# Cluster attention with gated projection on one core: paired sums of weight tiles on GpSimd, single-input work on ScalarE, and scaling straight out of the accumulator

## The chip, the cores and the metric

The kernel runs on one core of a Trainium2 chip. A core has five engines that run side by side, each through its own list of instructions in order: TensorE (matmuls and weight loads), VectorE, ScalarE, GpSimd and SyncE, which here issues the DMAs. They wait for one another by semaphores. The metric is the time of the program on the device in microseconds, lower is better; each execution gives one time. The program on record before the change was run three times.

## What is computed

Four batches, eight heads each, 768 positions, 64 features a head. Queries and keys are assigned to the nearest of 16 centroids; a query attends only to keys of its own cluster. The heads' outputs, put side by side (512 wide), go through a causal convolution of five taps whose sigmoid gates a projection, and a second projection gives the result.

```python
scores = scale * np.matmul(q, k.transpose(0, 1, 3, 2))
scores = np.where(mask, scores, -1000000000.0)
attn = np.exp(scores - np.max(scores, axis=-1, keepdims=True))
attn = attn / (np.sum(attn, axis=-1, keepdims=True) + 1e-09)
x = np.matmul(attn, v)                      # then heads side by side
gate = 1.0 / (1.0 + np.exp(-gate_pre))      # gate_pre: 5-tap convolution of x
out = gate * (x @ w_val) @ w_out
```

## The kernel before

**Heads and pairs.** There are 32 heads, worked on as 16 pairs, four to a batch. A head's scores are 768 x 768, made in six tiles of 128 keys x 768 queries. Each float operand is split into a high and a low part (`prep_x2`, `prep_x1` for one side, `prep_y1`, `prep_y2` for the other, L473 to L508) so that TensorE's faster float format is exact enough; the cluster one-hot rows lie in the low part and put the mask into the scores.

**A tile's way.** `qk` (L550) makes a score tile in PSUM (two buffers, `sp`). VectorE takes a maximum over each row (`rowmax`, L574), ScalarE the exponential (`expo`, L581), with the first tile's maximum as the shift for the whole head; the result is a weight tile `pt` of 128 x 768 floats in SBUF, one of 16 buffers. Two uses follow. `av` (L698) multiplies it with the values into an accumulator, both heads of a pair side by side, two banks a pair (one for each half of the queries). `sum_p` (L621) multiplies it with a block of weights 32 columns wide to get the row sums: one *set* is four matmuls, one for each head and half. `GROUPS` (L831) says which tiles a set covers; a group of two tiles is first added by `add_p` (L614) on GpSimd, into a buffer `ad`. Before the change every group has one tile, so no adds run and a pair has six sets. `weigh` and `weigh_v` (L588, L610) undo the shift between the keys' tiles by scaling the values.

**Scaling.** `av_out` (L711) copies the two banks of attention sums to `xr` on ScalarE and so frees them. `sum_out` (L635) copies the row sums out; a DMA gathers them (`sum_spread`), VectorE takes the reciprocals (`recip`), one DMA writes them to DRAM (`recip_row`) and two bring them back across partitions (`recip_rows`, tile `rs`). `scale_x` (L715) multiplies `xr` by `rs` on GpSimd. The last pair goes another way, over TensorE transposes.

**After the attention.** `post_x` and `post_xl` split x in high and low, `post_conv` (L730) does the five taps, the first on ScalarE or GpSimd (`scaled`), the other four on VectorE. `val` and `proj` (L780, L805) are the projections, which run on TensorE between the attention's matmuls; those of the last batch come at the end. The two weight matrices are decoded in the first part of the run (`load_w1`, `load_w3`).

**The order.** All instructions are in hand-made order: a planner written in Python (L829 to L1267) builds a list of operations `Op` with an engine (or a choice of engines, for the kinds in `FLEX`), a duration, predecessors, buffers to take and a due time, and simulates the engines greedily. Only the order and the choice of engine and buffer come out of it; on the chip the semaphores decide when each instruction runs. PSUM has four banks of the kind `acc`, shared by attention accumulators, row sums, projections and small transposes. When GpSimd and certain VectorE operations (`PORT`, L847) overlap in the plan, both are lengthened by `CLASH` = 0.8 of the overlap. TensorE's rule (L1179 on) prefers score tiles, up to three in a row, then alternates between bursts of attention products and of projections; sets of sums go ahead of attention products.

**The end.** A flag tells whether the fast path was exact enough; the program then branches over `general_path` (L1314), which these inputs don't take.

Of the kernel before, what the change touches and what calls it, by code (L numbers as in the profile page):

```python
# [14 lines left out]
ALU = mybir.AluOpType  # L15
# [139 lines left out]
def kernel(  # L155
# [12 lines left out]
    PE, V, S, G = nc.tensor, nc.vector, nc.scalar, nc.gpsimd  # L168

    NH, D, SQ = qT.shape  # L170
# [3 lines left out]
    NP = HB // 2  # L174
# [325 lines left out]

    def prep_y2(h, i):

        if ops[h][3] is None:
            ops[h][3] = operand(h, 3)
        y2 = ops[h][3]
        c = slice(i * HALF, (i + 1) * HALF)
        n = P if h < 2 else D
        (V if on[0] == "V" else G).tensor_tensor(y2[0:n, c], raws["k", h][0:n, c], ops[h][2][0:n, c].bitcast(F32), op=ALU.subtract)  # L508
# [206 lines left out]
    def scale_x(p, hf):  # L715
        if hf is None:
            x = xrs[p % 3][:, KW - 1:KW - 1 + SQ]
            G.tensor_tensor(x, x, sums.pop(p), op=ALU.mult)  # L718
        else:
            x = xrs[p % 3][:, KW - 1 + hf * HALF:KW - 1 + (hf + 1) * HALF]  # L720
            V.tensor_tensor(x, x, sums.pop((p, hf))[:, 0:HALF], op=ALU.mult)

# [48 lines left out]
    FLEX = ("X2", "Y1", "W1", "W3", "XF", "MQ", "PX", "PC0", "VS")  # L771
    CLASH = 0.8


# [54 lines left out]
    NS = 2 * NT  # L829
    NPT, NAD = 16, 4  # L830
    GROUPS = [[(t,) for t in range(NT)] for p in range(NPAIR)]  # L831
    NTILE = NH * NT
# [18 lines left out]
    class Op:  # L851
        def __init__(o, kind, eng, dur, f, *a, after=(), take=None, dl=None, lo=0, key=0):
            o.kind, o.engs, o.f, o.a = kind, eng if isinstance(eng, dict) else {eng: dur}, f, a
            if len(o.engs) > 1 and kind not in FLEX:
                o.engs = {"G": o.engs["G"]} if "G" in o.engs else {"V": o.engs["V"]}
            o.port = kind in PORT
            o.after = [x for x in after if x is not None]
            o.take, o.dl, o.lo, o.key, o.n = take, dl, lo, key, len(todo)
            o.end, o.got, o.users, o.on, o.free = None, 0, [], None, None
            todo.append(o)  # L860
# [67 lines left out]
    X1 = [Op("XF", {"G": 1.75, "V": 0.5}, 0, prep_x1_first, 1, hf * HALF, (hf + 1) * HALF, after=[X2], dl=2 + 5 * hf) for hf in range(2)]  # L928
    Y2 = [Op("Y2", "G", 0.97, prep_y2, 1, hf, after=[Y1], dl=2) for hf in range(2)]
    x10 = Op("X1", "V", 0.5, prep_x1, 0, HALF, SQ, dl=4)  # L930
# [22 lines left out]
    for h in range(2, NH):  # L953
# [6 lines left out]
        X1 = Op("X1", "V", 0.88, prep_x1, h, after=[X2], dl=s - 5).frees(LQ)  # L960
        Y2 = Op("Y2", "G", 0.97, prep_y2, h, 0, after=[Y1], dl=s - 5)
        Y2 = Op("Y2", "G", 0.97, prep_y2, h, 1, after=[Y2], dl=s - 5).frees(LK)
        ready[h] = [X1, Y2]

# [53 lines left out]
    for p in range(NPAIR):  # L1018
# [20 lines left out]
        prev.frees(LV[p])  # L1039
        for hf in range(2):  # L1040
            AVO[p, hf] = Op("AO", "A", 0.375, av_out, p, hf, after=[AVK[p, hf, NT - 1]], dl=-1).frees(AVK[p, hf, 0])
        LE = Op("LE", "A", 0.42, sum_out, p, after=[LL[p, len(GROUPS[p]) - 1]], take="lr", dl=-1).frees(LL[p, 0])
        if p < NPAIR - 1:
# [3 lines left out]
            RS = dma("RS", recip_rows, p, after=[RR], take="rs", dl=0).frees(RR)  # L1047
            SX[p, 0] = SX[p, 1] = Op("SX", "G", 1.65, scale_x, p, None, after=[AVO[p, 0], AVO[p, 1], RS], dl=-1).frees(RS)
        else:
            LT = Op("RT", "P", 0.33, sum_t, p, after=[LE], take="acc", dl=-1).frees(LE)  # L1050
            RQ = Op("RC", "V", 0.35, recip_q, p, after=[LT], dl=-1).frees(LT)
            late.append(LT)
            for hf in range(2):
                RB = Op("RB", "G", 0.6, recip_b, p, hf, after=[RQ], take="st", dl=-1)
                RT = Op("RT", "P", 0.33, recip_t, p, hf, after=[RB], take="acc", dl=-1).frees(RB)
                SX[p, hf] = Op("SV", "V", 0.46, scale_x, p, hf, after=[AVO[p, hf], RT], dl=-1).frees(RT)
# [82 lines left out]
    free = {"P": 0.0, "V": -0.2, "A": -0.2, "G": -0.6, "S": 0.5}  # L1139
    running = {"V": None, "G": None}  # L1140
    state = {"qk": 0, "since": 0, "last": None, "run": 0, "open": None}
# [10 lines left out]
    def est(o, e):  # L1152
# [6 lines left out]
        if o.take:  # L1159
# [3 lines left out]
            t = max(t, f[0])  # L1163
        return t

# [49 lines left out]
    while left:  # L1215
# [13 lines left out]
        T = max(T, est(o, e))  # L1229
        dur = o.engs[e]  # L1230
        if e == "P":

# [18 lines left out]
        o.start = T  # L1251
        if e in running:
            x = running["G" if e == "V" else "V"]
            if (o.port or e == "G") and x is not None and (x.port or x.on == "G") and x.free > T:
                m = CLASH * min(x.free - T, dur)
                dur, x.free, x.end, free[x.on] = dur + m, x.free + m, x.end + m, free[x.on] + m
            running[e] = o
        free[e] = o.free = T + dur
# [38 lines left out]
    prep_first2(0, 0)  # L1297
    prep_y2(0, 0)
    on[0] = "V"
    prep_y2(0, 1)  # L1300
    for t in range(2):
        qk(0, t, True)
    warm(WARM[3])
    for i, hf, e in ((0, 0, "A"), (1, 0, "V"), (1, 1, "V")):
        on[0] = e
        prep_mask0(0, i, hf)
    for o in order:
        got[0], on[0] = o.got, o.on
        o.f(*o.a)
# [3 lines left out]
    ctx.close()  # L1313
    with tc.If(rv != 0, preferred_fallthrough_block=False):  # L1314
        general_path(tc, qT, kT, v, out, cenT, cw, wsplit, ident)
# [39 lines left out]
```

## Time and profile before

| what | us |
|---|---|
| median of three runs | 588.81 |
| lowest and highest of them | 587.38, 590.2 |
| the profiled execution: its own time | 589.81 |
| the profiled execution: its span, first to last instruction | 588.1 |
| mean granted TensorE clock, share of full | 0.963 |

The profile shows one execution. *Busy* is the time in which an engine executes something; a matmul's end is modelled, and matmuls overlap. A row of a group gives line, engine, operation, tiles and shape, count, then busy time in us and mean duration in ns, then the idle time just before and what ended it. A row of waits says who waited for whom, us in total, how often, longest. A row of windows gives, for a stretch of the span, the busy time of each engine with the count of instructions, the granted clock, the DMA engines' share and GB/s. "PEld" is the weight load, a "q" behind an engine's name its sequencer. Where a line gathers several forms, a mean mixes them.

### The profile page before, as it was taken

The numbers are of one execution on the slowest core, as the hardware profiler recorded it, in microseconds if no ns is written. First come the engines' busy times: TensorE is split into PE (matmuls) and PEld (weight loads), VectorE is DVE, ScalarE is ACT, GpSimd is POOL, SyncE is SP. The second block draws the span as 40 slices with busy tenths as digits, with TensorE's granted clock in tenths as the row PEclk, the third lists the DMA queues.
The fourth block names the chain that finished last, engine by engine and source line by source line (L and its number), as shares of the span: only waits on it lengthen the run. The fifth ranks groups of instructions, "written<-read, shape, count | busy, mean of one in ns | idle before, by whom it ended". The sixth has DMA issues, their size and how long they took to land. (4 is left out here: it accounts for less than half of the span.)

```text
span 588.1 us, 8869 instructions
## 1 busy us (share of the span) xinstructions
PE 540.1 (92%) x3235; PEld 342.3 (58%) x3235; DVE 411.7 (70%) x582; ACT 298.8 (51%) x436; POOL 270.8 (46%) x268
## 2 busy tenths in 40 slices
PE   7787698979899999999999999999999999999893
PEld 4434444455466664756556656766576667655792
DVE  5787879899789679658958682898658555905610
ACT  4635545464544445657555545556456535532321
POOL 5516414846624546663445541567254422244520
PEclk9799589989889999999999999999999999999997
DMA  8934346253822363435533443325323321000001
GB/s 217 260 120 110 104 122 185 79 139 89 226 61 69 99 213 104 135 93 159 148 85 116 129 130 114 114 87 167 118 60 113 92 71 46 28 20 36 19 36 59
DMA packets 35295, 64.27 MB, mean 109 GB/s; under 512 B 9772, under 2 KB 18092, under 8 KB 35244
## 3 DMA queue, kind: packets, MB, share of 16 engines
q1 hardware_dynamic: 35244, 63.63, 37.9%
q8 instruction: 27, 0.44, 0.3%
q14 instruction: 24, 0.20, 0.1%
HBM read 54.19 MB, written 6.38 MB: 103 GB/s over the span
## 5 line engine op out<-in xcount | busy, mean ns | idle before, releaser
L577 DVE TENSOR_REDUCE nmx<-sp 128x1 f32<-128x768 f32 x192 | 177.7, 949 | 88.2 <-PE sp L563 72.1
L584 ACT ACTIVATE pt<-sp,nmx 128x768 f32<-128x768 f32 x192 | 165.9, 899 | 132.4 <-DVE nmx L579 42.2
L704 PE MATMUL acc<-pt,vt 128*64 128x384 f32 x768 | 138.4, 495 | 0.0
L558 PE MATMUL sp<-op,op 128*128 128x384 f32 x372 | 109.3, 376 | 16.2 <-ACT pt L584 9.3
L736 DVE SCALAR_TENSOR_TENSOR gate<-xr,cw,gate 128x768 f32<-128x768 f32 (+1 forms) x84 | 90.1, 1093 | 25.0 <-ACT gate L214 21.6
L563 PE MATMUL sp<-op,op 80*128 80x384 f32 (+1 forms) x372 | 100.2, 352 | 0.0
L558 PEld LDWEIGHTS sp<-op,op 128*128 128x128 f32 x372 | 64.8, 196 | 56.6 <-ACT pt L584 23.1
L704 PEld LDWEIGHTS acc<-pt,vt 128*64 128x64 f32 x768 | 49.3, 136 | 69.5 <-issue 67.7
L508 POOL TENSOR_TENSOR op<-raw,op 64x384 fp32r<-64x384 f32 (+1 forms) x62 | 77.4, 1262 | 7.5 <-ACT op L214 5.1
L630 PE MATMUL acc<-pt,wt 128*32 128x384 f32 x768 | 73.3, 511 | 4.0 <-ACT pt L584 2.2
L563 PEld LDWEIGHTS sp<-op,op 80*128 80x128 f32 (+1 forms) x372 | 71.4, 198 | 0.0
L803 POOL TENSOR_TENSOR h<-gate,h 128x384 fp32r<-128x384 f32 x32 | 34.8, 1095 | 61.7 <-ACT h L799 61.6
L216 POOL TENSOR_SCALAR op<-raw,qsc 128x768 fp32r<-128x768 f32 x26 | 24.9, 959 | 79.2 <-PE sp L563 76.4
L718 POOL TENSOR_TENSOR xr<-xr,rs 128x768 f32<-128x768 f32 x15 | 27.7, 1850 | 68.4 <-ACT xr L713 64.7
L812 PE MATMUL acc<-wh_o,h 128*128 128x512 f32 x144 | 49.5, 403 | 0.0
L482 DVE SCALAR_TENSOR_TENSOR op<-raw,op 128x768 fp32r<-128x768 f32 (+1 forms) x31 | 46.0, 1484 | 1.5 <-ACT op L214 0.7
L630 PEld LDWEIGHTS acc<-pt,wt 128*32 128x32 f32 x768 | 21.7, 113 | 41.8 <-issue 32.0
L787 PE MATMUL acc<-xh,wh_v 128*128 128x384 f32 x96 | 33.8, 352 | 0.3 <-ACT oh L460 0.3
L728 POOL TENSOR_TENSOR xl<-xr,xh 128x768 fp32r<-128x768 f32 (+1 forms) x21 | 33.7, 1618 | 0.4
L812 PEld LDWEIGHTS acc<-wh_o,h 128*128 128x128 f32 x144 | 27.1, 188 | 11.2 <-issue 3.7
L787 PE MATMUL acc<-xl,wh_v 128*128 128x384 f32 x96 | 32.5, 338 | 0.0
L787 PE MATMUL acc<-xh,wl_v 128*128 128x384 f32 x96 | 32.4, 338 | 0.0
(160 smaller groups left out, 594.2 us busy)
## 6 DMA issues: line engine op xcount, KB each, us to landing
raw<-kT SPq DMA_DIRECT2D x62, 192.0 KB
raw<-qT SPq DMA_DIRECT2D x62, 192.0 KB
sraw<-kT SPq DMA_DIRECT2D x32, 192.0 KB
sraw<-qT SPq DMA_DIRECT2D x32, 192.0 KB
vt<-v SPq DMA_DIRECT2D x16, 384.0 KB
out_dram<-ob SPq DMA_DIRECT2D x24, 256.0 KB
rs<-rr SPq DMA_DIRECT2D x30, 192.0 KB
op<-oht SPq DMA_DIRECT2D x56, 48.0 KB
```

Source lines behind the costliest of these rows:

```text
L482: V.scalar_tensor_tensor(x1[:, c0:c1], raws["q", h][:, c0:c1], QS, x2[:, c0:c1], op0=ALU.mult, op1=ALU.subtract)
L508: (V if on[0] == "V" else G).tensor_tensor(y2[0:n, c], raws["k", h][0:n, c], ops[h][2][0:n, c].bitcast(F32), op=ALU.subtract)
L558: PE.matmul(sp[:, hf, 0:HALF], x1[:, ts_], y1[:, hf * HALF:(hf + 1) * HALF], start=True, stop=False)
L563: PE.matmul(sp[:, hf, 0:HALF], x2[0:KR, ts_], y2[0:KR, hf * HALF:(hf + 1) * HALF], start=False, stop=True)
L577: V.tensor_reduce(out=nm, in_=sp[:, :, 0:HALF], op=ALU.max, axis=AX.XY, negate=True)
L584: S.activation(o.rearrange("p (a b) -> p a b", a=2), sp[:, :, 0:HALF], AF.Exp, bias=nmx[:, h, 0:1], scale=1.0)
L630: PE.matmul(lacc[p][32 * u:32 * u + 32, 0:HALF], wts[p][:, e], x[:, hf * HALF:(hf + 1) * HALF], start=(g == 0), stop=(g == len(GROUPS[p]) ...
L704: PE.matmul(acc[e * D:(e + 1) * D, 0:HALF], vt[:, j, e * D:(e + 1) * D], pts[2 * p + e, j][:, hf * HALF:(hf + 1) * HALF], start=(j == 0), ...
L736: V.scalar_tensor_tensor(g, xr[:, k + c0:k + c1], cw[:, ct, k:k + 1], g, op0=ALU.mult, op1=ALU.add)
L787: PE.matmul(macc[b, ch, m][:, 0:HALF], a[:, kt, ms], x[:, kt, cs], start=(kt == 0 and i == 0), stop=(kt == NC - 1 and i == 2))
L803: G.tensor_tensor(hl[:, m], gate[:, m, ch * HALF:(ch + 1) * HALF], hh[:, m].bitcast(F32), op=ALU.subtract)
L812: PE.matmul(macc[b, ch, t][:, 0:DM], x[:, kt, ts_], a[:, kt, :], start=(kt == 0 and i == 0), stop=(kt == NC - 1 and i == 2))
```

## The change

- **Sums.** For pairs 0 to 3 everything stays; from the fifth pair on `GROUPS` becomes (0,1), (2,3), (4,), (5,): GpSimd adds two couples of tiles a head, and TensorE has four sets. The buffers are cut anew: 13 weight tiles and 3 sums, where there were 16 weight tiles and no sums in use.
- **Scaling.** For all pairs but the last, `av_out` and GpSimd's product go; VectorE multiplies the accumulator by the reciprocals and writes `xr`, one instruction for each half. The bank is freed by that product.
- **Engines.** Operations of the kinds X2, Y1, PX, PC0, VS and W3 that may run on ScalarE now always do.
- **Y2.** The low part of an operand is one GpSimd instruction of 768 columns, no longer two of 384 (heads 2 on).
- **The planner.** GpSimd's operations and VectorE's of the kinds in `PORT` now take turns on one resource; the lengthening by `CLASH` goes.
- **The end.** The general path becomes the branch's fall-through, and a hint, placed 60 operations before the end of the list on all engines, names the likely jump.

```diff
-    def prep_y2(h, i):
+    def prep_y2(h, c0, c1):
...
-        if hf is None:
-            x = xrs[p % 3][:, KW - 1:KW - 1 + SQ]
-            G.tensor_tensor(x, x, sums.pop(p), op=ALU.mult)
+        x = xrs[p % 3][:, KW - 1 + hf * HALF:KW - 1 + (hf + 1) * HALF]
+        if (p, hf) in sums:
+            V.tensor_tensor(x, x, sums.pop((p, hf))[:, 0:HALF], op=ALU.mult)
         else:
...
+            V.tensor_tensor(x, avacc.pop((p, hf))[:, 0:HALF], sums[p][:, hf * HALF:(hf + 1) * HALF], op=ALU.mult)
...
-    CLASH = 0.8
...
-    NPT, NAD = 16, 4
-    GROUPS = [[(t,) for t in range(NT)] for p in range(NPAIR)]
+    NPT, NAD = 13, 3
+    GROUPS = [[(t,) for t in range(NT)] if p < NP else [(0, 1), (2, 3), (4,), (5,)] for p in range(NPAIR)]
...
+            if kind in ("X2", "Y1", "PX", "PC0", "VS", "W3") and "A" in o.engs:
+                o.engs = {"A": o.engs["A"]}
...
-        Y2 = Op("Y2", "G", 0.97, prep_y2, h, 0, after=[Y1], dl=s - 5)
-        Y2 = Op("Y2", "G", 0.97, prep_y2, h, 1, after=[Y2], dl=s - 5).frees(LK)
+        Y2 = Op("Y2", "G", 1.65, prep_y2, h, 0, SQ, after=[Y1], dl=s - 5).frees(LK)
...
-        for hf in range(2):
-            AVO[p, hf] = Op("AO", "A", 0.375, av_out, p, hf, after=[AVK[p, hf, NT - 1]], dl=-1).frees(AVK[p, hf, 0])
...
-            SX[p, 0] = SX[p, 1] = Op("SX", "G", 1.65, scale_x, p, None, after=[AVO[p, 0], AVO[p, 1], RS], dl=-1).frees(RS)
+            for hf in range(2):
+                SX[p, hf] = Op("SX", "V", 0.46, scale_x, p, hf, after=[AVK[p, hf, NT - 1], RS], dl=-1).frees(RS)
+                SX[p, hf].frees(AVK[p, hf, 0])
...
-    running = {"V": None, "G": None}
+    port = [0.0]
...
-        return t
+        return max(t, port[0]) if needs_port(o, e) else t
+
+    def needs_port(o, e):
+        return e == "G" or e == "V" and o.port
...
+        if needs_port(o, e):
+            port[0] = T + dur
...
-        if e in running:
-            x = running["G" if e == "V" else "V"]
-            if (o.port or e == "G") and x is not None and (x.port or x.on == "G") and x.free > T:
-                m = CLASH * min(x.free - T, dur)
-                dur, x.free, x.end, free[x.on] = dur + m, x.free + m, x.end + m, free[x.on] + m
-            running[e] = o
...
-    for o in order:
+    for n, o in enumerate(order):
+        if n == len(order) - 60:
+            tc.mark_branch_hint_location(
+                "general", "LikelyTaken", [getattr(mybir.EngineType, e) for e in ("SP", "PE", "DVE", "Activation", "Pool")]
+            )
...
-    with tc.If(rv != 0, preferred_fallthrough_block=False):
+    with tc.If(rv != 0, preferred_fallthrough_block=True, label="general"):
```

The adds themselves are `add_p`, which stood in the kernel before without being called: `G.tensor_tensor(o, pts[h, a], pts[h, b], op=ALU.add)`, planned at 1.65 us with a due time of three tiles after the second tile.

More of the change, by code (lines that the diff above doesn't have):

```diff
@@ L505, in prep_y2 @@
         y2 = ops[h][3]
-        c = slice(i * HALF, (i + 1) * HALF)
+        c = slice(c0, c1)
         n = P if h < 2 else D
@@ L715, in scale_x @@
     def scale_x(p, hf):
-        if hf is None:
-            x = xrs[p % 3][:, KW - 1:KW - 1 + SQ]
-            G.tensor_tensor(x, x, sums.pop(p), op=ALU.mult)
-        else:
-            x = xrs[p % 3][:, KW - 1 + hf * HALF:KW - 1 + (hf + 1) * HALF]
-            V.tensor_tensor(x, x, sums.pop((p, hf))[:, 0:HALF], op=ALU.mult)
+        x = xrs[p % 3][:, KW - 1 + hf * HALF:KW - 1 + (hf + 1) * HALF]
+        if (p, hf) in sums:
+            V.tensor_tensor(x, x, sums.pop((p, hf))[:, 0:HALF], op=ALU.mult)
+        else:
+            V.tensor_tensor(x, avacc.pop((p, hf))[:, 0:HALF], sums[p][:, hf * HALF:(hf + 1) * HALF], op=ALU.mult)
     def post_x(p, c0, c1):
@@ L928 @@
     X1 = [Op("XF", {"G": 1.75, "V": 0.5}, 0, prep_x1_first, 1, hf * HALF, (hf + 1) * HALF, after=[X2], dl=2 + 5 * hf) for hf in range(2)]
-    Y2 = [Op("Y2", "G", 0.97, prep_y2, 1, hf, after=[Y1], dl=2) for hf in range(2)]
+    Y2 = [Op("Y2", "G", 0.97, prep_y2, 1, hf * HALF, (hf + 1) * HALF, after=[Y1], dl=2) for hf in range(2)]
     x10 = Op("X1", "V", 0.5, prep_x1, 0, HALF, SQ, dl=4)
@@ L1053 @@
             for hf in range(2):
+                AVO[p, hf] = Op("AO", "A", 0.375, av_out, p, hf, after=[AVK[p, hf, NT - 1]], dl=-1).frees(AVK[p, hf, 0])
                 RB = Op("RB", "G", 0.6, recip_b, p, hf, after=[RQ], take="st", dl=-1)
@@ L1297 @@
     prep_first2(0, 0)
-    prep_y2(0, 0)
+    prep_y2(0, 0, HALF)
     on[0] = "V"
-    prep_y2(0, 1)
+    prep_y2(0, HALF, SQ)
     for t in range(2):
```

## The prediction

> **What bounds the kernel now.** I read the views in this order: the page's first part, the windows by stage, the waits of each engine in the long stage, then the groups of the lines that the change touches. The chain of waits consists of the last copy alone, so it names no bound and is not used.
>
> ```profile
> span 588.1 us, 8869 instructions
> PE 540.1 (92%) x3235; PEld 342.3 (58%) x3235; DVE 411.7 (70%) x582; ACT 298.8 (51%) x436; POOL 270.8 (46%) x268
> ```
>
> ```profile
> 72.00:108.00 36.00, 32.05 (x215) 15.75 (x215) 29.77 (x46) 19.19 (x28) 13.18 (x13) 0.94 0.49 133
> 108.00:144.00 36.00, 32.21 (x186) 18.53 (x184) 33.98 (x40) 21.10 (x29) 25.62 (x19) 0.91 0.40 109
> 144.00:180.00 36.00, 33.19 (x192) 20.30 (x189) 29.80 (x46) 18.94 (x29) 15.93 (x17) 0.91 0.50 131
> 180.00:576.00 396.00, 386.32 (x2334) 254.02 (x2334) 265.43 (x365) 201.75 (x299) 182.89 (x162) 1.00 0.33 97
> 576.00:588.00 12.00, 2.89 (x13) 2.00 (x11) 0.00 (x0) 1.20 (x2) 0.00 (x0) 0.74 0.14 50
> ```
>
> The columns after the length are busy time of matmuls, weight loads, VectorE, ScalarE and GpSimd, then the granted clock. There are two stages. From 72 to 180 us VectorE is busy 93.6 of 108 us (86.6%), and TensorE idles 10.5 us (9.8%) at a clock below 1. From 180 to 576 us TensorE is busy 386.3 of 396 us, with 9.7 us idle (2.4%), full clock, and VectorE at 67.0%. In that stage the waits, here of TensorE, VectorE and ScalarE, point the same way:
>
> ```profile
> PE sp L558 <- ACT pt L584: 2.6, 6, 0.8
> ```
> ```profile
> DVE nmx L577 <- PE sp L563: 59.6, 31, 6.6
> ```
> ```profile
> ACT pt L584 <- PE acc L704: 21.8, 20, 3.1
> ```
>
> The longest wait of TensorE's matmuls is 2.6 us in 396; VectorE waits 59.6 us for score tiles from TensorE, and ScalarE's exp waits 21.8 us until an attention product has freed a weight tile. TensorE is the bound there: a microsecond of its work is about a microsecond of the span.
>
> **The sums that go.** Each pair of heads had six sets of row sums on TensorE (L630), four matmuls each, recorded as eight. From the fifth pair on there are four sets: 12 pairs lose two each, 24 sets.
>
> ```profile
> 144.00:180.00 36.00, 5.19 (x48) 1.50 (x48) 0.91 0.50 131
> 180.00:576.00 396.00, 47.97 (x528) 14.48 (x528) 1.00 0.33 97
> ```
> ```profile
> 323.10 2.79 PE L630 MATMUL acc<-pt,wt 128*32 128x384 f32 x32
> ```
>
> These are the windows of L630 alone, and one burst of the timeline. 48 and 528 records are 6 and 66 sets, exactly the 72 of pairs five to sixteen: 5.19/6 = 0.865 us and 47.97/66 = 0.727 us a set. The burst has four sets in 2.79 us, 0.70 each. Removing 22 sets of the long stage and 2 before it is 22 x 0.727 + 2 x 0.865 = 17.7 us by averages, and 24 x 0.70 = 16.7 us by the burst. I take **-16.7 us**, since an average also holds the drain at a burst's end, which stays.
>
> **What GpSimd gets and gives.** Two adds a head for 24 heads are 48 instructions of 128x768; the same shape stands in the product with the reciprocals that leaves it (L718).
>
> ```profile
> L718 POOL TENSOR_TENSOR xr<-xr,rs 128x768 f32<-128x768 f32 x15 | 27.7, 1850 | 68.4 <-ACT xr L713 64.7 <-ACT pt L584 2.8 <-DMA rs<-rr 0.8
> L508 POOL TENSOR_TENSOR op<-raw,op 64x384 fp32r<-64x384 f32 x60 | 75.5, 1270 | 7.4 <-ACT op L214 5.1 <-PE acc L425 0.8 <-DMA raw<-kT 0.6
> L216 POOL TENSOR_SCALAR op<-raw,qsc 128x768 fp32r<-128x768 f32 x26 | 24.9, 959 | 79.2 <-PE sp L563 76.4 <-DMA raw<-kT 2.8
> L216 POOL TENSOR_SCALAR op<-raw 128x768 fp32r<-128x768 f32 x14 | 12.1, 865 | 4.7 <-DMA raw<-qT 2.9 <-PE sp L558 1.8
> L216 POOL TENSOR_SCALAR vt<-vt,wt 128x384 f32<-128x384 f32 x16 | 10.6, 662 | 45.6 <-DVE wt L608 45.6
> L216 POOL TENSOR_SCALAR xh<-xr 128x384 fp32r<-128x384 f32 (+1 forms) x15 | 9.8, 663 | 5.6 <-PE acc L787 5.1
> L216 POOL TENSOR_SCALAR gate<-xr,cw 128x768 f32<-128x768 f32 (+1 forms) x6 | 5.7, 952 | 6.4 <-DVE flag L762 6.0
> L214 ACT ACTIVATE op<-raw 128x768 fp32r<-128x768 f32 x17 | 14.3, 840 | 5.2 <-issue 2.6 <-DMA raw<-qT 1.5 <-PE sp L558 1.1
> L214 ACT ACTIVATE op<-raw,qsc 128x768 fp32r<-128x768 f32 x5 | 4.7, 935 | 3.4 <-issue 2.3 <-PE sp L563 1.1
> L713 ACT ACTIVATE xr<-acc 128x384 f32<-128x384 f32 x32 | 15.4, 490 | 7.2 <-PE acc L704 7.1
> L721 DVE TENSOR_TENSOR xr<-xr,acc 128x384 f32<-128x384 f32 x2 | 1.1, 554 | 2.7 <-ACT xr L713 2.7
> ```
>
> GpSimd: +48 x 1.85 = 88.8 us; -27.7 us of products; -63.1 us for the L216 groups shown; and 60 half differences of 1.27 us become 30 whole ones. No whole one is in the trace: between 1.27 (twice the width at no cost) and 2.54; I take L718's 1.85, so 76.2 - 55.5 = 20.7 us less. Sum: 270.8 + 88.8 - 27.7 - 63.1 - 20.7 = 248 us. GpSimd is not emptied, it is about as busy as before, and has no place on the bound.
>
> ScalarE: the 26 and 14 operand copies cost 26 x 0.935 + 14 x 0.840 = 36.1 us there, the other three groups about what they cost on GpSimd (26 us), and 30 copies of the attention sums go: 30 x 0.490 = 14.7 us. 298.8 + 36 + 26 - 15 = 346 us, some 60% of the span. The copies stand in line before exps, each for up to 0.93 us; they are hidden as long as TensorE has other work than scores, and that cover is what the friction below prices.
>
> VectorE: two products of 0.554 us for 15 pairs, +16.6 us; four pairs of it (4.4 us) fall in the early stage. They read the attention sums where TensorE left them, so two of four accumulator banks are now held until the reciprocals have landed. That wait is added, and behind it in VectorE's line stand the row maxima of the next tiles. Rows of one pair:
>
> ```profile
> 245.59 1.16 SPq L663 DMA_DIRECT2D rs<-rr x2
> ```
> ```profile
> 264.60 0.49 ACT L637 ACTIVATE lr<-acc 128x384 f32<-128x384 f32 x1 [1.82 <-PE acc L630]
> 265.38 1.69 ACT L584 ACTIVATE pt<-sp,nmx 128x768 f32<-128x768 f32 x2 [0.28 <-PE acc L704]
> 270.31 2.80 PE L704 MATMUL acc<-pt,vt 128*64 128x384 f32 x16
> 271.37 1.71 ACT L584 ACTIVATE pt<-sp,nmx 128x768 f32<-128x768 f32 x2 [1.01 <-DVE nmx L577]
> 273.54 1.84 POOL L718 TENSOR_TENSOR xr<-xr,rs 128x768 f32<-128x768 f32 x1 [10.50 <-ACT xr L713]
> ```
>
> The broadcast of the seventh pair's reciprocals is issued at 245.6 us; its product starts at 273.5, released by the attention copy. The reciprocals are some 27 us early, so I cost the bank's hold at nothing in the long stage; without that cover it would be the exchange from the sums' copy to the broadcast. The DMAs and their order on SP are the same as before in number. The path from attention product to scaled x loses a copy of 0.49 us and a GpSimd product of 1.84 us against two VectorE products of 0.554 us; it is not late, so nothing is counted.
>
> **Two couplings get tighter.** Weight tiles go from 16 buffers to 13, and the hand planner now treats GpSimd and part of VectorE's work as one resource. In the rows above the eighth pair's copy of sums is at 264.6, the ninth pair's first exps run at 265.4 and 271.4, the eighth pair's attention products start around 270.3: about four exps pass before tiles come free, which is the spare of 16 over the pair's 12. With 13 the spare is one. TensorE then has to take attention products earlier, or the exps stop while it does something else. What that costs TensorE isn't in the trace, so it is bounded: below by 0. For the upper end I use the two stages: TensorE's idle share is 2.4% at 67.0% VectorE and 9.8% at 86.6%. VectorE in the long stage becomes (265.4 + 11 pairs x 1.11)/(396 - 16) = 73.0%, on the line between the two 4.7% idle, 17.7 us against 9.7: +8 us. I take the middle, **+4 us**, as nothing is nearer to either end.
>
> GpSimd's adds lie beside VectorE's two-input work:
>
> ```profile
> L482 DVE SCALAR_TENSOR_TENSOR op<-raw,op x31: 519/1541/4631, 17.5 to 481.0; 128x768 fp32r<-128x768 f32 x30, 128x384 fp32r<-128x384 f32 x1
> L736 DVE SCALAR_TENSOR_TENSOR gate<-xr,cw,gate x84: 547/1009/2929, 72.8 to 551.7; 128x768 f32<-128x768 f32 x44, 128x384 f32<-128x384 f32 x40
> ```
>
> Minimum, median and maximum in ns: one instruction takes from 1.5 to 4.6 us at the same 768 columns, so something holds these lines up. [...] The long stage holds 28 us of L482's and 68 us of L736's work beside 131 us of idle VectorE, so the sum doesn't change.
>
> **The end.** The branch over the general path is turned round and hinted.
>
> ```profile
> 579.60 0.33 SPq L822 DMA_DIRECT2D out_dram<-ob  x1
> ```
> ```profile
> L1314 SPq COMPARE_BRANCH  x2: 38/46/53, 580.6 to 582.9; - x2
> ```
> ```profile
> L1351 SPq EVENT_SEMAPHORE  x10: 17/28/28, 585.7 to 588.0; - x10
> ```
>
> After the last store SP branches a second time at 582.9 us and does its next instruction at 585.7: 2.7 us of nothing. If the target is already there these go; otherwise they stay. A hint is one more sequencer step an engine, like the branches of 38 to 53 ns, below 0.1 us. I take **-2.7 us**, bounds 0 and -2.7.
>
> **Sum.** -16.7 - 2.7 + 4 = -15.4 us. Span 588.1 becomes 572.7; the profiled execution's own time, 589.8 us, becomes 574.4. It stands 1.0 us above the median of the runs (588.81), so the forecast is **573.4 us**.
>
> **Rivals.**
>
> *Better, 566.4 us.* With 63 us of single-input work off GpSimd and a plan that keeps it from VectorE's two-input lines, the early stage shortens as well. In the windows from 36 to 180 us L482 takes 15.57 us for 9 and L736 22.56 us for 20:
>
> ```profile
> 36.00:180.00 144.00, 15.57 (x9) 0.89 0.42 115
> ```
> ```profile
> 36.00:180.00 144.00, 22.56 (x20) 0.89 0.42 115
> ```
>
> Nine at their median-like 1.0 us of L736 save 6.6 us; the four pairs' products cost 4.4; with some 0.8 us from L736, -3 us, and no friction: -16.7 - 2.7 - 3 = -22.4.
>
> *Half lost, 581 us.*
>
> ```profile
> L718 POOL TENSOR_TENSOR xr<-xr,rs x15: 1805/1833/2139, 61.5 to 530.0; 128x768 f32<-128x768 f32 x15
> ```
>
> The tighter couplings cost the full +8 us, and the 24 sets that now wait for adds stand in TensorE's line by half of what L718's longest (2139 ns) is over its shortest (1805 ns): 24 x 0.17 = 4 us. -16.7 - 2.7 + 12 = -7.4. For it: VectorE's 86.6% in the early stage came with 9.8% idle TensorE. Against it: ScalarE and VectorE wait on TensorE, not the reverse, for 81 us of the long stage.
>
> *Hidden anyway, 586.1 us.* TensorE isn't really full, because matmuls overlap; the sums then were hidden, and only the end's 2.7 us show. The windows' weight loads speak for it: 254 of 396 us, 64%. [...] The burst of 32 matmuls in 2.79 us, 87 ns each with no gaps, and 2.6 us as longest wait speak against it.
>
> *Slower, 598.0 us.* The 13 weight tiles decide.
>
> ```profile
> L584 ACT ACTIVATE pt<-sp,nmx x192: 876/901/909, 16.3 to 515.1; 128x768 f32<-128x768 f32 x192
> ```
>
> 192 exps start between 16.3 and 515 us, one each 2.6 us. If at each of the 11 changes of pair in the long stage one such interval finds TensorE with neither an attention product nor a projection to do, 11 x 2.6 = 28.6 us come in: -19.4 + 28.6 = +9.2. It decides from 19.4/11 = 1.8 us a change on. For it: exps already wait 21.8 us for tiles. Against it: with exps blocked TensorE turns to the attention products, which are what frees the tiles.
>
> **How the numbers follow.** Chances: forecast 0.55, better 0.12, half lost 0.14, hidden 0.08, slower 0.11. A measurement of this kernel can tell about 0.5% from no change, 585.9 to 591.8 us. Faster: 0.55 + 0.12 + 0.14 = 0.81; within: 0.08; slower: 0.11. The range goes from 564 us (somewhat past the better case, whose size is uncertain by the 1.0 us more of averages and the friction) to 587 us, which holds the hidden case; the slower case and the far ends of the others are left out, under 2 in 10.
>
> **What would show it.** Right: L630 with 576 records for 768 and about 55 us for 73.3; 48 adds near 1.85 us; TensorE busy near 520 us and idle below 5% after 180 us; SP's end within 6 us of the last store. Wrong: TensorE idle over 25 us in the long stage, with waits of L558 on exps (tiles) or of L630 on GpSimd adds; VectorE waiting on the broadcast of reciprocals; or an end still 8.5 us behind the last store.

## The result, and the profile after

| | us |
|---|---|
| changed kernel: median of four runs | 569.48 |
| lowest and highest of them | 567.57, 570.71 |
| the kernel before in the same comparison | 589.14 |
| ratio, with its 95% interval | 0.967 [0.963, 0.971] |
| the profiled execution: its own time, its span | 570.32, 568.5 |

The changed kernel is faster by 19.7 us (3.3%). The forecast was 573.4: the direction and most of the size came true, and 3.9 us more came than were counted. In the tables below, runs over 1.5% above the fastest of their kernel are left out of a median: three of six in e6 (595.12 with all six) and three of six in e11 (586.50 with all six).

The page's first part, for the changed kernel:

```profile
span 568.5 us, 8493 instructions
PE 529.5 (93%) x3043; PEld 338.3 (60%) x3043; DVE 420.8 (74%) x611; ACT 341.3 (60%) x488; POOL 249.9 (44%) x190
```

TensorE's busy time fell by 10.6 us (540.1 to 529.5) and the rest of the span, in which it does nothing, by 9.0 us (48.0 to 39.0). So the 19.6 us of span come about half and half from less busy time of TensorE and from less waiting. The groups of the changed kernel, with the shapes kept apart, show the work:

```profile
L617 POOL TENSOR_TENSOR ad<-pt,pt 128x768 f32<-128x768 f32 x48 | 92.8, 1933 | 104.4 <-ACT pt L584 92.8 <-PE acc L630 6.6 <-DMA sraw<-qT 2.6
L508 POOL TENSOR_TENSOR op<-raw,op 64x768 fp32r<-64x768 f32 x30 | 57.4, 1915 | 79.2 <-ACT op L214 78.9 <-PE acc L704 0.2
L630 PE MATMUL acc<-pt,wt 128*32 128x384 f32 x384 | 39.2, 522 | 0.0
L630 PE MATMUL acc<-ad,wt 128*32 128x384 f32 x192 | 21.1, 512 | 0.1
L720 DVE TENSOR_TENSOR xr<-acc,rs 128x384 f32<-128x384 f32 x30 | 16.0, 548 | 6.6 <-DMA rs<-rr 2.6 <-PE acc L704 2.3 <-issue 1.6
```

The 48 adds take 1.93 us each, a whole low part (L508) 1.92 us. The sums (L630) have 384 + 192 = 576 records, where there were 768. Their two rows can't be added up, because within a burst the two kinds overlap in time; two rows of the timeline show it:

```profile
257.44 0.85 PE L630 MATMUL acc<-ad,wt 128*32 128x384 f32 x8
258.12 0.83 PE L630 MATMUL acc<-pt,wt 128*32 128x384 f32 x8
```

The windows of L630 alone count such time once. Before, then after (matmuls, weight loads, clock, DMA share, GB/s):

```profile
0.00:180.00 180.00, 25.30 (x240) 7.22 (x240) 0.90 0.52 140
180.00:560.00 380.00, 47.97 (x528) 14.48 (x528) 1.00 0.34 99
```
```profile
0.00:180.00 180.00, 23.87 (x224) 6.77 (x224) 0.88 0.51 143
180.00:560.00 380.00, 34.20 (x352) 8.59 (x352) 1.00 0.34 100
```

So the sums fall from 73.3 to 58.1 us, by 15.2. TensorE's other work grew from 466.8 to 471.4 us, by 4.6.

The products on VectorE (L720) wait 2.6 us in all for the reciprocals' broadcast, and no wait of TensorE names them: the accumulator bank that is now held longer holds nobody up. The windows by stage (matmuls, weight loads, VectorE, ScalarE, GpSimd, then granted clock, DMA share, GB/s) show where the waiting went. Before:

```profile
0.00:36.00 36.00, 27.40 (x176) 16.61 (x176) 24.68 (x52) 19.22 (x28) 16.40 (x46) 0.91 0.88 240
36.00:72.00 36.00, 26.00 (x128) 15.06 (x128) 28.06 (x38) 17.38 (x25) 16.81 (x15) 0.83 0.32 88
```

After:

```profile
0.00:36.00 36.00, 30.41 (x190) 17.77 (x190) 25.23 (x56) 22.73 (x32) 13.28 (x42) 0.91 0.89 240
36.00:72.00 36.00, 30.37 (x163) 17.15 (x165) 28.67 (x40) 22.73 (x31) 11.01 (x7) 0.81 0.39 109
72.00:180.00 108.00, 97.05 (x553) 55.61 (x546) 91.63 (x142) 66.33 (x93) 39.25 (x25) 0.89 0.43 122
180.00:556.00 376.00, 364.19 (x2117) 242.19 (x2116) 275.31 (x376) 227.41 (x330) 185.30 (x116) 1.00 0.35 100
```

In the first 72 us TensorE is busy 60.8 us, where it was 53.4: 7.4 us less waiting, in a stretch before the first paired sum. Not all of that is gained: up to 180 us it is 7.0 us busier (157.8 for 150.8) at a clock of 0.88 for 0.90, and has done 897 records for 891, or 22 more if the sums are left aside. From 72 to 180 us its idle time is 10.95 us, as before (10.6). In the long stage it is 11.8 of 376 us (3.1%), 2 us more than before, and VectorE is at 73.2%.

The end shrank too. The timeline's row of the last store and the rows of the line after the branch, for the changed kernel:

```profile
564.21 0.33 SPq L819 DMA_DIRECT2D out_dram<-ob  x1
```
```profile
L1316 SPq COMPARE_BRANCH  x1: 70/70/70, 565.2 to 565.2; - x1
```
```profile
L1316 SPq EVENT_SEMAPHORE  x8: 17/17/17, 565.7 to 567.1; - x8
```
```profile
L1353 SPq EVENT_SEMAPHORE  x10: 17/28/28, 567.2 to 568.4; - x10
```

From the last store's issue to the end of the span it is 4.3 us; before it was 8.5 (579.6 to 588.1). The 2.7 us without an instruction on SP are gone (the next one starts 0.5 us after the branch), and the closing round of semaphores takes 1.2 us, where it took 2.3.

### The profile page after: what moved, and what is told of

Read it like the earlier page. It is cut to its first block, busy times and chain, and to the rows that moved or that the text cites. A ratio compares the mean times of both kernels' runs of the same rounds, so it can differ in the third digit from the quotient of the medians.

```text
span 568.5 us, 8493 instructions
## 1 busy us (share of the span) xinstructions
PE 529.5 (93%) x3043; PEld 338.3 (60%) x3043; DVE 420.8 (74%) x611; ACT 341.3 (60%) x488; POOL 249.9 (44%) x190
## 5 line engine op out<-in xcount | busy, mean ns | idle before, releaser
L704 PE MATMUL acc<-pt,vt 128*64 128x384 f32 x768 | 140.4, 498 | 0.0
L617 POOL TENSOR_TENSOR ad<-pt,pt 128x768 f32<-128x768 f32 x48 | 92.8, 1933 | 104.4 <-ACT pt L584 92.8
L558 PE MATMUL sp<-op,op 128*128 128x384 f32 x372 | 111.1, 381 | 17.1 <-ACT pt L584 14.8
L508 POOL TENSOR_TENSOR op<-raw,op 64x768 fp32r<-64x768 f32 (+1 forms) x32 | 59.7, 1868 | 79.2 <-ACT op L214 78.9
L704 PEld LDWEIGHTS acc<-pt,vt 128*64 128x64 f32 x768 | 49.1, 137 | 73.3 <-issue 67.0
L735 DVE SCALAR_TENSOR_TENSOR gate<-xr,cw,gate 128x768 f32<-128x768 f32 (+1 forms) x84 | 83.7, 1012 | 1.2 <-ACT gate L214 0.4
L482 DVE SCALAR_TENSOR_TENSOR op<-raw,op 128x768 fp32r<-128x768 f32 (+1 forms) x31 | 51.5, 1662 | 4.8 <-ACT op L214 4.7
L800 POOL TENSOR_TENSOR h<-gate,h 128x384 fp32r<-128x384 f32 x32 | 35.4, 1113 | 40.0 <-ACT h L796 40.0
L809 PE MATMUL acc<-wh_o,h 128*128 128x512 f32 x144 | 49.4, 401 | 0.0
L727 POOL TENSOR_TENSOR xl<-xr,xh 128x768 fp32r<-128x768 f32 (+1 forms) x21 | 31.8, 1520 | 32.8 <-ACT xh L214 28.5
L630 PE MATMUL acc<-pt,wt 128*32 128x384 f32 x384 | 39.2, 522 | 0.0
L796 ACT ACTIVATE h<-gate 128x384 fp32r<-128x384 f32 x32 | 16.0, 520 | 30.4 <-DVE gate L790 30.1
L809 PEld LDWEIGHTS acc<-wh_o,h 128*128 128x128 f32 x144 | 27.0, 188 | 9.7 <-issue 1.8
L214 ACT ACTIVATE op<-raw,qsc 128x768 fp32r<-128x768 f32 x31 | 28.8, 930 | 4.5 <-PE sp L563 4.2
```

Of the source, the lines that this page charges most:

```text
L482: V.scalar_tensor_tensor(x1[:, c0:c1], raws["q", h][:, c0:c1], QS, x2[:, c0:c1], op0=ALU.mult, op1=ALU.subtract)
L558: PE.matmul(sp[:, hf, 0:HALF], x1[:, ts_], y1[:, hf * HALF:(hf + 1) * HALF], start=True, stop=False)
L617: G.tensor_tensor(o, pts[h, a], pts[h, b], op=ALU.add)
L630: PE.matmul(lacc[p][32 * u:32 * u + 32, 0:HALF], wts[p][:, e], x[:, hf * HALF:(hf + 1) * HALF], start=(g == 0), stop=(g == len(GROUPS[p]) ...
L704: PE.matmul(acc[e * D:(e + 1) * D, 0:HALF], vt[:, j, e * D:(e + 1) * D], pts[2 * p + e, j][:, hf * HALF:(hf + 1) * HALF], start=(j == 0), ...
L735: V.scalar_tensor_tensor(g, xr[:, k + c0:k + c1], cw[:, ct, k:k + 1], g, op0=ALU.mult, op1=ALU.add)
```

## The experiments

Each ratio is to runs of the kernel before on the same chip; their medians are 588.9 to 589.4 us, so medians can be compared across the rows. "Busy" is TensorE's busy time in the profiled execution, "rest" that execution's span less it: everything in which TensorE does nothing, the end included (the profiled executions lie within 3 us of these medians). "P" marks paired sums, "M" the moved parts (scaling on VectorE, copies on ScalarE, whole low parts, the planner's turns), "E" the new end; the digits are the weight tiles.

| kernel | parts | median us | ratio to before [95%] | busy | rest |
|---|---|---|---|---|---|
| before | 16 | 588.81 | 1 | 540.1 | 48.0 |
| changed | P M E 13 | 569.48 | 0.967 [0.963, 0.971] | 529.5 | 39.0 |
| e1 | E 16 | 585.70 | 0.994 [0.992, 0.996] | 542.2 | 41.4 |
| e2 | P 13 | 595.91 | 1.012 [1.009, 1.015] | 534.5 | 60.1 |
| e3 | M E 16 | 593.00 | 1.007 [1.004, 1.010] | 548.1 | 42.9 |
| e4 | M E 13 | 585.02 | 0.993 [0.991, 0.996] | 544.9 | 37.0 |
| e5 | as changed, copies free to choose | 580.69 | 0.986 [0.982, 0.991] | 533.8 | 44.2 |
| e6 | as changed, scaling as before | 590.78 | 1.003 (on record 1.010 [1.005, 1.015]) | 533.4 | 53.2 |
| e7 | as changed, planner without turns | 592.05 | 1.006 [1.004, 1.009] | 533.1 | 56.5 |
| e8 | as changed, all pairs paired | 601.66 | 1.020 [1.016, 1.023] | 535.4 | 62.7 |
| e9 | as changed, another order | 608.74 | 1.034 [1.032, 1.037] | 542.7 | 64.3 |
| e10 | P 13, another order | 577.67 | 0.980 [0.976, 0.983] | 527.8 | 48.5 |
| e11 | as changed, couples of other tiles and another order | 583.71 | 0.990 (on record 0.986 [0.981, 0.992]) | 533.8 | 50.8 |
| e12 | as changed, another order | 584.71 | 0.992 [0.989, 0.995] | 532.3 | 51.3 |

### One part alone

**e1, the end alone**, on the kernel before:

```diff
+    for n, o in enumerate(order):
+        if n == len(order) - 60:
+            tc.mark_branch_hint_location("general", "LikelyTaken", ...)
-    with tc.If(rv != 0, preferred_fallthrough_block=False):
+    with tc.If(rv != 0, preferred_fallthrough_block=True, label="general"):
```

> The kernel before with the branch turned round and hinted, nothing else. Theory (the end is a step of its own, and it was under-sized at 2.7 us: the profiles show 8.5 us from the last store to the last instruction before and about 4.3 after): 4.2 us faster, 585 us, ratio 0.993, with the same order of work up to the last store. Rival (the shorter end of the changed kernel comes from its other order, not from the branch): within 1 us of 589.

Measured: 3.5 us faster than before. Its last store is issued at 579.15 us of a span of 583.6, so the tail is 4.4 us for 8.5. The end is a part of its own, and worth somewhat more than its 2.7 us, because the closing round of semaphores is shorter as well. The gap of 2.7 us goes with the turned and hinted branch: in e1 SP branches at 580.1 us and its next instruction starts at 580.6. What SP does in the gap of the kernel before, no run here shows.

The run doesn't tell the hint from the turned branch. And the traces have the hint elsewhere than the program's text: the only hint of each engine runs at the start of the span, 564 us ahead of the branch in the changed kernel (579 us in e1), not 60 operations before the end. SP's row of the changed kernel:

```profile
L1353 SPq BRANCH_PREFETCH_HINT  x1: 51/51/51, 0.8 to 0.8; - x1
```

**e2, the paired sums alone**, on the kernel before:

```diff
-    NPT, NAD = 16, 4
-    GROUPS = [[(t,) for t in range(NT)] for p in range(NPAIR)]
+    NPT, NAD = 13, 3
+    GROUPS = [[(t,) for t in range(NT)] if p < NP else [(0, 1), (2, 3), (4,), (5,)] for p in range(NPAIR)]
```

> The kernel before with the paired sums alone (13 weight tiles, 3 sums, four sets from the fifth pair on); GpSimd keeps all it had and gets 48 adds more, some 360 us of work. Theory (TensorE is the bound and the sums are worth their time there whatever else GpSimd does): 13 to 17 us faster, 572 to 576 us. Rival (the gain needs the emptied GpSimd: with it full, sets of sums wait for adds and operands are late): under 6 us faster or slower than before, TensorE waiting for GpSimd in the long stage by over 10 us more.

**e3, everything but the sums and the tiles**, on the changed kernel:

```diff
-    NPT, NAD = 13, 3
-    GROUPS = [... if p < NP else [(0, 1), (2, 3), (4,), (5,)] for p in range(NPAIR)]
+    NPT, NAD = 16, 4
+    GROUPS = [[(t,) for t in range(NT)] for p in range(NPAIR)]
```

> The changed kernel with six sets for all pairs and 16 weight tiles: all of the change but the sums. Theory (sums worth 13 to 17 us of the 19.7, the end 4): 583 to 586 us. Rival (moved work and the planner's turns bring most of it): under 578 us. Third possibility (what is moved costs by itself, and the sums gain more than 17): over 587 us.

**e4, the same with 13 tiles**: `GROUPS` as in e3, `NPT, NAD = 13, 3` kept.

> As e3, but with 13 weight tiles in place of 16: the price of the three tiles alone. Theory (they cost TensorE nearly nothing, because attention products are taken earlier): within 3 us of e3. Rival, as in the prediction's slower case (one exp interval at each change of pair): 10 to 28 us slower than e3.

Measured: e2 is 1.2% slower than before although TensorE has 5.6 us less to do; its rest grew by 12.1 us. The obvious reading was that GpSimd is too full without the moved parts (343.1 us busy, 58%); e10 below takes it away. e3 is slower than e1 by 7.3 us, and e4, with three weight tiles *fewer*, is faster than e3 by 8.0 us, which neither of its expectations had. A smaller ring of tiles can't help by itself: what differs is the order that the planner makes from it. So 13 tiles have no price of their own that these runs could show.

The nearest pair is e4 and the changed kernel: the same tiles, the same engines, the same end, and only `GROUPS` differs. With it the planner writes another order here too, but the rest is nearly equal. The first part of the page and the sums' group of e4:

```profile
PE 544.9 (94%) x3235; PEld 343.6 (59%) x3235; DVE 411.0 (71%) x613; ACT 340.7 (59%) x486; POOL 157.5 (27%) x142
```
```profile
L630 PE MATMUL acc<-pt,wt 128*32 128x384 f32 x768 | 75.1, 514 | 1.5 <-DVE wt L608 1.0 <-ACT pt L584 0.5
```

From e4 to the changed kernel the sums go from 75.1 to 58.1 us, TensorE's busy time from 544.9 to 529.5 (-15.4) and the rest from 37.0 to 39.0, so the profiled span falls by 13.4; the medians fall by 15.5 (585.02 to 569.48), as e4's profiled execution lies 1.4 us below its median and the changed kernel's 0.8 above. GpSimd takes 92 us more. VectorE takes 9.8 us more, nearly all in its two lines beside the adds, L482 and L735 (126.0 to 135.2 us), and the time doesn't show it. Where the rest stays about the same, then, most of each microsecond off TensorE is off the time.

### One part of the change undone

**e5** lets the copies choose between ScalarE and GpSimd again:

```diff
-            if kind in ("X2", "Y1", "PX", "PC0", "VS", "W3") and "A" in o.engs:
-                o.engs = {"A": o.engs["A"]}
```

> The changed kernel with the choice between GpSimd and ScalarE given back to the planner for X2, Y1, PX, PC0, VS and W3. Theory (from e2 to e4: the sums pay only where GpSimd has been relieved, since attention and convolution steps behind a full GpSimd are late): GpSimd some 300 us busy, 576 to 585 us. Rival (relief by the other two parts is enough): within 3 us of the changed kernel's 569.5.

**e6** scales as before, copies on ScalarE and one product on GpSimd:

```diff
+        for hf in range(2):
+            AVO[p, hf] = Op("AO", "A", 0.375, av_out, p, hf, ...).frees(AVK[p, hf, 0])
...
-            for hf in range(2):
-                SX[p, hf] = Op("SX", "V", 0.46, scale_x, p, hf, ...).frees(RS)
-                SX[p, hf].frees(AVK[p, hf, 0])
+            SX[p, 0] = SX[p, 1] = Op("SX", "G", 1.65, scale_x, p, None, ...).frees(RS)
```

> The changed kernel with the scaling back as it was: two copies on ScalarE and one product of 1.85 us on GpSimd, 28 us of GpSimd in all. Theory (relief of GpSimd in general decides, and this is the smaller part of it): 572 to 578 us. Rival (the shorter way from attention product to scaled x, through VectorE alone, decides): over 580 us. Second rival (neither matters): within 2 us of 569.5.

**e7** plans with the lengthening of 0.8 of the overlap in place of the turns:

```diff
-        return max(t, port[0]) if needs_port(o, e) else t
+        return t
...
-        if needs_port(o, e):
-            port[0] = T + dur
...
+                m = 0.8 * min(x.free - T, dur)
```

> The changed kernel with the planner's old rule for GpSimd beside VectorE (both lengthened by 0.8 of their overlap) in place of taking turns. Only the order changes. Theory (turns keep long runs of GpSimd away from VectorE's two-input work, so without them that work is held up longer): VectorE's two-input lines 10 us or more longer in sum, 573 to 580 us. Rival (the order rule does nothing on the chip, as the semaphores decide): within 2 us of 569.5.

**e8** pairs the sums from the first pair on:

```diff
-    GROUPS = [[(t,) for t in range(NT)] if p < NP else [(0, 1), (2, 3), (4,), (5,)] for p in range(NPAIR)]
+    GROUPS = [[(0, 1), (2, 3), (4,), (5,)] for p in range(NPAIR)]
```

> The changed kernel with paired sums for the first four pairs too: 16 adds more, 8 sets fewer. Theory (TensorE is not the bound before 180 us, where VectorE is busy 84% and TensorE idles): 0 to 2 us faster than 569.5 or slower by the adds' 30 us of GpSimd beside VectorE's decoding, up to 4 us. Rival (sets are worth their time anywhere): 5 to 6 us faster, 564 us.

Measured: 11, 21, 23 and 32 us slower than the changed kernel. Read as prices, the three undone parts alone would be worth 55 us, nearly three times what the whole change brings; and e8, which takes 64 records from TensorE, has a *longer* busy time than the changed kernel (535.4 for 529.5). So they can't be prices. What the four have in common is that each makes the planner write another order. In e7 the two VectorE lines do take 9.4 us longer than in the changed kernel (144.6 for 135.2), about what was expected, but TensorE's rest is 17.5 us longer, so that isn't the whole of it.

### Another order of the same work

e9 and e12 change one number of the planner each and leave the work as it is (up to three small instructions move between ScalarE and VectorE); e10 is e2 with three such numbers changed; e11 couples other tiles, with two.

```diff
-    TOL = {"V": 0.3, "A": 0.3, "G": 2.0}
+    TOL = {"V": 0.2, "A": 0.3, "G": 2.0}
```

> The changed kernel with one number of the planner altered: the tolerance with which VectorE's less urgent work may hold up urgent work, 0.2 us for 0.3. Same instructions, another order, which the planner itself holds to be some 15 us longer. Theory (what e5 to e8 showed is mostly the order that the planner happened to find, TensorE's work being the same): 580 to 595 us, TensorE busy within 4 us of the changed kernel's 529.5, idle up by 12 us or more. Rival (the parts undone in e5 to e8 have prices of their own, and order alone is worth little): within 4 us of 569.5.

```diff
-    TOL = {"V": 0.3, "A": 0.3, "G": 2.0}
-    AHEAD = 20
+    TOL = {"V": 0.35, "A": 0.3, "G": 1.5}
+    AHEAD = 17
...
-                AD[h, g] = Op("AD", "G", 1.65, add_p, h, g, ...)
+                AD[h, g] = Op("AD", "G", 1.7, add_p, h, g, ...)
```

> e2 (paired sums alone, GpSimd full) with three numbers of the planner altered, chosen so that the planner finds a shorter order: VectorE's tolerance 0.35, GpSimd's 1.5, look-ahead of the assignment's loads 17, the add planned at 1.7. Theory (e2 lost by its order): 575 to 585 us, faster than before. Rival (adds on a full GpSimd cost more than the sums save, whatever the order): over 588 us, idle of TensorE as high as e2's 50 us.

```diff
-    TOL = {"V": 0.3, "A": 0.3, "G": 2.0}
+    TOL = {"V": 0.3, "A": 0.25, "G": 1.5}
...
-    GROUPS = [... else [(0, 1), (2, 3), (4,), (5,)] for p in range(NPAIR)]
+    GROUPS = [... else [(0,), (1, 2), (3, 4), (5,)] for p in range(NPAIR)]
```

> The changed kernel with the couples (1,2) and (3,4) in place of (0,1) and (2,3), and tolerances of 0.25 for ScalarE and 1.5 for GpSimd: the same count of sets and adds, in an order that the planner holds to be some 2 us shorter. Theory (sets are worth the same whichever tiles are added; order decides the rest): 565 to 575 us. Rival (the first set of a pair must come late, and tile 0 alone helps it to start early): 560 to 565 us.

```diff
-    AHEAD = 20
+    AHEAD = 16
```

> The changed kernel with the look-ahead of the assignment's loads at 16 for 20, the planner's own end being the same. Theory (the planner's end tells most of the chip's time): 566 to 574 us. Rival (the chip's contention, which the planner knows roughly, spreads equal plans widely): 575 us or more.

Measured: the same work takes 569.5, 584.7 (e12) or 608.7 us (e9). And the paired sums alone take 595.9 or 577.7 us (e10), the latter with GpSimd just as full as in e2:

```profile
PE 527.8 (92%) x3043; PEld 336.3 (58%) x3043; DVE 424.3 (74%) x582; ACT 311.6 (54%) x456; POOL 344.4 (60%) x296
```

So e2 lost by its order, and GpSimd at 344 us doesn't keep the sums' gain from showing: e10, with the old end and none of the moved parts, is 11.7 us faster than before. The moved parts aren't needed for the gain; whether they add to it is open, since e1 to e4 is within 0.7 us and e1 to e3 is 7.3 us the other way. None of the orders tried beats the changed kernel. Of the four runs only e10 came out as its theory said: e9, e11 and e12 took longer than expected, e12 by 11 us although the planner's own end was unchanged. So the planner's end tells the chip's time only roughly.

### What a bad order does

The largest losses have one hole in common, near 260 to 290 us, where the ninth pair's exps begin. The timeline of e9 (start, length, what, in brackets the engine's idle time before and what ended it):

```profile
260.35 0.90 ACT L584 ACTIVATE pt<-sp,nmx 128x768 f32<-128x768 f32 x1 [6.01 <-DVE nmx L579]
...
270.61 3.90 POOL L800 TENSOR_TENSOR h<-gate,h 128x384 fp32r<-128x384 f32 x4 [0.63 <-ACT h L796]
...
282.81 4.63 POOL L800 TENSOR_TENSOR h<-gate,h 128x384 fp32r<-128x384 f32 x4 [8.30 <-ACT h L796]
284.83 14.55 DVE L735 SCALAR_TENSOR_TENSOR gate<-xr,cw,gate 128x768 f32<-128x768 f32 x12 [14.56 <-ACT gate L214]
293.51 2.80 PE L704 MATMUL acc<-pt,vt 128*64 128x384 f32 x16
295.07 1.69 ACT L584 ACTIVATE pt<-sp,nmx 128x768 f32<-128x768 f32 x2
```

One exp at 260.35, the next at 295.07: 33.8 us without any. With 13 weight tiles, the eighth pair's twelve and this one fill the ring, and a tile comes free only when the eighth pair's attention products (L704) run. The planner puts these behind the convolution of the fifth pair (L735), which shares their buffer of x (three buffers, pairs three apart); and the convolution writes the gate tile that the first batch's gated projection still reads (L800). So the first batch's last projections (L809) come before them in TensorE's list. TensorE takes its list in order, and from 270.6 to 293.5 us it works through 72 records of these projections, which need L800 too; the first of them waits 4.4 us for L796, ScalarE's step before L800. The products themselves wait for nothing then; the row of their first weight loads:

```profile
293.51 0.20 PEld L704 LDWEIGHTS acc<-pt,vt 128*64 128x64 f32 x4 [0.36 <-issue]
```

So on the chip it is TensorE's own list that holds the products, and with them the exps; the convolution has its part in it only by the plan. In the changed kernel the same steps are early; its timeline:

```profile
246.44 1.75 POOL L800 TENSOR_TENSOR h<-gate,h 128x384 fp32r<-128x384 f32 x1
...
255.32 1.96 DVE L735 SCALAR_TENSOR_TENSOR gate<-xr,cw,gate 128x768 f32<-128x768 f32 x2
...
259.77 1.70 ACT L584 ACTIVATE pt<-sp,nmx 128x768 f32<-128x768 f32 x2 [1.25 <-PE acc L704]
...
264.83 2.16 PE L704 MATMUL acc<-pt,vt 128*64 128x384 f32 x12
266.77 0.89 ACT L584 ACTIVATE pt<-sp,nmx 128x768 f32<-128x768 f32 x1
```

The same four moments, read from each kernel's timeline (the line numbers are the changed kernel's; in e2, e6 and e10 these operations stand a few lines further on):

| kernel | last L800 of the first batch ends | fifth pair's convolution ends | eighth pair's products start | longest stop of the exps there |
|---|---|---|---|---|
| changed | 248.2 | 257.3 | 264.8 | 5.4 |
| e11 | 270.8 | 274.7 | 276.2 | 12.0 |
| e10 | 256.6 | 260.2 | 263.2 | 15.1 |
| e6 | 267.6 | 270.3 | 273.7 | 23.4 |
| e2 | 276.1 | 278.8 | 282.6 | 25.0 |
| e8 | 278.5 | 281.2 | 284.6 | 27.3 |
| e9 | 287.4 | 290.1 | 293.5 | 33.8 |

In each of the six with the hole the products start 1.5 to 3.8 us after the convolution, and the convolution ends 2.7 to 3.9 us after the gated projection. But in all seven the products' first weight load shows under 0.7 us of idle time, put down to issue. What lengthens with the hole is the number of projection records that TensorE takes in it: 33 in e11, 37 in e10, 60 in e2, 71 in e6 and 72 in e8 and e9, for 6 in the changed kernel. That the plan puts the products so late because of the buffer of x is read from the program; a fourth buffer, which would show it, wasn't tried. e5, e7 and e12 have no such hole, and their 11 to 23 us stay open: their idle time lies in many short waits of TensorE, the longest 4.3 us.

The hole costs less than its length, because TensorE has those projections to do meanwhile; but the clock is lower there. The windows of this stretch, e9 and then the changed kernel:

```profile
252.00:324.00 72.00, 55.76 (x256) 35.20 (x257) 46.43 (x51) 31.91 (x50) 28.95 (x21) 0.81 0.26 80
```
```profile
252.00:324.00 72.00, 65.92 (x377) 42.76 (x376) 61.56 (x77) 43.88 (x64) 34.41 (x20) 0.98 0.37 105
```

TensorE is 10.2 us less busy and does 256 records for 377, at a clock of 0.81 for 0.98. The projections' rows show it directly: from one `wl_o` matmul to the next, three matmuls on, it is 1.28 us at first and 0.70 a little later; the granted clock was 0.67 from 262 to 272 us, 0.82 from 272 to 282 and 1.00 from 282 to 293.

```profile
272.70 0.63 PE L809 MATMUL acc<-wl_o,h 128*128 128x512 f32 x1
273.98 0.63 PE L809 MATMUL acc<-wl_o,h 128*128 128x512 f32 x1
276.11 0.40 PE L809 MATMUL acc<-wl_o,h 128*128 128x512 f32 x1
276.81 0.39 PE L809 MATMUL acc<-wl_o,h 128*128 128x512 f32 x1
```

So part of e9's busy time of 542.7 us, 13.2 more than the changed kernel's, is the same work at a lower clock. These slower matmuls come after waits of 5.5 us (to 261.3) and 4.4 us (to 270.6); whether the waits are what lowers the clock, no run here shows.

## Why the prediction was right, and where not

- **TensorE is the bound: right.** From e4 to the changed kernel 15.4 us less of busy time went with 13.4 us less of span, and from before to e10 12.3 us with 11.8. That settles the rival "hidden anyway": TensorE's matmuls were busy 97.6% of the long stage and its weight loads 64%, and the matmuls' busy share told where the gain would be.
- **The sums, -16.7 us: right, somewhat large.** Against the kernel before the group falls by 15.2 us; against e4 by 17.0. In the long stage the 22 sets brought 13.8 us (47.97 to 34.20), 0.63 each. The forecast took the burst's 0.70 so as to leave the drain behind, but the 44 sets that stay went from 0.727 to 0.777 us each, which gives back 2.2: bursts got shorter, and one of a single set takes 0.85 us (the row at 257.44), where the burst of four takes 2.79.
- **TensorE's other work, 0: a term without a line in the sum.** It took 4.6 us more. The clock up to 180 us is lower (0.88 for 0.90) with more records done; how much of the 4.6 us that explains isn't settled.
- **GpSimd and ScalarE: right.** Estimated 248 and 346 us busy, measured 249.9 and 341.3; an add taken as 1.85 us is 1.93, a whole low part 1.92. Neither stands in the way.
- **The hold of the banks, 0: right in this order**, 2.6 us of wait in all, and not on TensorE. In other orders TensorE's matmuls do wait for these products (L720): 3.8 us in e7, 2.4 in e3, 2.1 in e12.
- **The end, -2.7: mis-sized.** e1 measures -3.5 and the tails -4.2. What was left out is the closing round of semaphores, 1.1 us shorter. That the gap goes because the target is already there was the author's guess; the runs show only that it goes.
- **Friction of the tighter couplings, +4, and the early stage, 0: the terms that failed.** The waits up to TensorE's last matmul fell: 7.4 us less in the first 72 us and 2.1 us more in the long stage, which alone is what the friction was about. There VectorE is busy 73.2%, as estimated (73.0%), and TensorE idles 3.1%, less than the 4.7% of the upper end. The first 72 us were not looked at: the prediction's early stage began at 36 us for two VectorE lines and at 72 us for TensorE, and there, from 72 to 180 us, indeed nothing changed. The moved parts can do it (e4: 30.80 + 30.37 us of TensorE's work in the first 72, e1 27.25 + 26.38), but an order alone does most of it too (e10: 26.65 + 32.02), so which it was in the changed kernel isn't settled.
- **The bounds of the friction, 0 to +8, were the real mistake.** The rest of the span is 39.0, 51.3 or 64.3 us for the same work, 25 us from end to end. Stating one value for "the tighter couplings" assumed that they have one. The outcome lies between the forecast and the rival "better", which had no friction and a shorter early stage.
- **The total: partly luck.** By its terms the forecast had 16.7 us less of TensorE's busy time and 1.3 us more of the rest; measured are 10.6 less and 9.0 less. Two errors, of 6 us and 10 us, cancel in part. The sign "TensorE busy near 520 us" failed (529.5), "about 55 us" of sums came near (58.1), and idle time below 5% and an end within 6 us held. With another order the same work would have missed the forecast by 11 or 35 us.
- **The slower rival was right in its mechanism and wrong in its place.** It let tiles stop the exps at each of 11 changes of pair by 2.6 us. In e9, e8, e2 and e6 the ring does stop the exps, for 23 to 34 us, but at one change, while TensorE takes a long run of projections ahead of the products. In the changed kernel few stand there, by the order it got.

## What to carry to other kernels

Where an engine is busy 97% of a stage and the others wait for it, price what leaves it from a dense burst, and what stays a little dearer. Where the order of the work comes from a planner, part of any change's result is the order that it happens to get: here the same work differs by 39 us, so undoing parts one by one prices nothing unless the two kernels are compared at equal idle time of the bounding engine, or over several orders each. And look at all stages for idle time of the bound, the first ones too.

## What the runs showed of the hardware

How long GpSimd can hold up VectorE was not expected. L482 reads two SBUF tiles. A row of the changed kernel's timeline, where GpSimd is idle from 260.40 to 262.27 us, and the line's row among its groups:

```profile
260.29 0.95 DVE L482 SCALAR_TENSOR_TENSOR op<-raw,op 128x768 fp32r<-128x768 f32 x1
```
```profile
L482 DVE SCALAR_TENSOR_TENSOR op<-raw,op 128x768 fp32r<-128x768 f32 x30 | 50.4, 1680 | 4.8 <-ACT op L214 4.7
```

Nearly undisturbed it takes 0.95 us, on average 1.68. In e2 one took 6.00 us. VectorE's row and GpSimd's in e2's timeline:

```profile
259.21 1.83 POOL L718 TENSOR_TENSOR xr<-xr,rs 128x768 f32<-128x768 f32 x1
259.59 6.00 DVE L482 SCALAR_TENSOR_TENSOR op<-raw,op 128x768 fp32r<-128x768 f32 x1 [0.74 <-ACT op L214]
261.00 1.97 POOL L508 TENSOR_TENSOR op<-raw,op 64x384 fp32r<-64x384 f32 x2
262.95 1.83 POOL L728 TENSOR_TENSOR xl<-xr,xh 128x768 fp32r<-128x768 f32 x1
```

Four GpSimd instructions follow one another without a gap from 259.21 to 264.78 us, and L482, begun at 259.59, ends at 265.59, 0.81 us after the last of them: nearly its whole undisturbed length. GpSimd's own took their usual time (1.83 us). So here VectorE's instruction was held until GpSimd paused, rather than both slowed: in these rows all of the contention is on VectorE's side.

It isn't always so. In the changed kernel an L482 that began at 393.35 us, beside an add from 392.72 to 394.56, took 2.03 us: it ended 0.82 us after the add, although GpSimd's next instruction had begun at 394.51. And GpSimd's instructions can take longer too: an add that began at 398.31, while an L735 ran until 399.27, took 2.67 us, where the median add takes 1.84. Why VectorE waits for four instructions in one case and for one in the other isn't shown. The row maxima, which read PSUM, take 950 ns on average in e4, where GpSimd is busy for 157.5 us, and 949 in e10, where it is busy for 344.4.
